# A linear-attention and gated-MLP kernel on one core: zeros by ScalarE, loads with their gaps, merged first loads, and a planner that counts instruction blocks

## The chip, the core and the metric

The kernel runs on one core of a Trainium2 chip. The core has five engines, each with its own queue of instructions, executed in order: TensorE (PE in the profile; its weight loads are shown as PEld), VectorE (DVE), ScalarE (ACT), GpSimd (POOL) and SyncE (SP), which here issues all copies between HBM and the on-chip memory. Engines wait for one another through semaphores. The metric is device time in microseconds, the median of several runs; lower is better.

## The reference

```python
for t in range(S):                      # S = 768, for 4 batches x 8 heads, head size 48
    kt, vt, bt = (k_n[:, :, t], v[:, :, t], beta[:, :, t, None])
    y[:, :, t] = np.einsum('bhd,bhde->bhe', q[:, :, t], state)
    v_old = np.einsum('bhde,bhd->bhe', state, kt)
    state = state + bt[:, :, :, None] * np.einsum('bhd,bhe->bhde', kt, vt - v_old)
...
x = attn_out.transpose(0, 2, 1, 3).reshape(B * S, H * D)     # 3072 tokens x 384
out = (x @ w_a * (x @ w_b)) @ w_out                          # 384 -> 1536 -> 384, float32
```

K is normalised per head and token. The first part is a recurrence over 768 tokens (a delta rule), the second a gated MLP without a non-linearity.

## The kernel before

**Tiling.** The 768 tokens are cut into 24 chunks of 32, and those into six groups of four. Within a chunk the recurrence is written as a triangular system, so that only 24 chunk steps are sequential. Four functions make the work of a group, and one that of the MLP:

- `weights(p)` loads a quarter or a half of the weights, which come as 64-bit floats, decodes them on VectorE to 32 bits (`decode`), takes a common scale from a Gram matrix on TensorE (`gram`, `total`), and splits each into two fp16 halves (`wsl`) or two F32R halves (`wo_hi`, `wo_lo`).
- `prep(g)` normalises K and scales, loads K and Q of a chunk with the feature dimension on partitions (`load_raw` into `raw0`, or into `raws`, a part of `wsl`, for the first group), multiplies by the norms (`rbk0`, which for later groups comes by way of a DRAM scratch `rk` and is spread over 64 partitions), splits into fp16 halves (`kqc`) and copies them into block matrices (`kqbd`).
- `solve(g)` inverts the triangular systems by elimination on VectorE, in tiles of the ring `b4` (one of which GpSimd clears first).
- `steps(g)` does the sequential steps: per chunk 48 + 24 + 48 + 24 tiny matmuls and 96 more that add to the state in the PSUM tile `S_ps`, with `tabd` as block matrix, and the chunk's tokens, split in fp16 halves, into `x`.
- `moe(s, ths)` does the MLP for a pair of chunks: 18 matmuls `bank<-x,wsl` of 256 columns, a product on VectorE (`g`), its split (`ghl`), and later 6 matmuls with `wo_hi` and `wo_lo`. This is most of TensorE's work; in this text it is the gated work.

The block matrices `kqbd` (4) and `tabd` (2) are zero outside their blocks. K and Q for two heads sit at partitions 0 to 47 and 64 to 111 of 112; the 16 between must be zero too. Before, GpSimd clears `raws`, three `kqbd` and both `tabd`, in 41 memsets, and VectorE the rest.

**The order.** Every operation is recorded in a list with an estimated duration (`price`), and `pack` simulates all engines: whenever an engine is free, it takes the ready operation of highest priority. That is done forwards and backwards in turn `PASSES` times, and the best order found is what each engine's queue then holds (`issue`, line 402, which is why nearly all rows of the profile have that line). `HOLD` lets a low-priority operation be held back for a short time for an urgent one. PSUM banks are given out by the same simulation. The estimated durations and the resulting order set everything; on the chip each engine follows its list.

Of the kernel before, what the change touches and what calls it, by code (L numbers as in the profile page):

```python
# [12 lines left out]
F32 = mybir.dt.float32  # L13
F32R = mybir.dt.float32r
F16 = mybir.dt.float16
I32 = mybir.dt.int32
# [6 lines left out]
B, H, S, D = 4, 8, 768, 48  # L23
DM, FF = 384, 1536
C = 32
NCH = S // C
P = 128
# [16 lines left out]


class Op:
    __slots__ = ("eng", "calls", "dur", "move", "rd", "wr", "deps", "pri", "at", "end", "tag", "stream", "banks", "cold", "use")

    def __init__(self, eng):
        self.eng, self.calls, self.dur, self.move = eng, [], 0.0, 0.0  # L50
        self.cold, self.use = 0.0, 0.0
        self.rd, self.wr, self.deps, self.tag, self.banks = {}, {}, set(), "", set()


class Plan:
# [89 lines left out]
    @staticmethod  # L145
    def price(eng, name, outs, ins, kw):
        out = outs[0]
        n = 1
        for d in out.shape[1:]:
            n *= d  # L150
        space = lambda a: getattr(a.tensor, "_space", None)
        wide = [a for a in ins if a.shape[-1] > 1 or len(a.shape) > 2]
        psum = any(space(a) == bass.MemoryType.PSUM for a in wide)
        if eng == "PE":
            k, m = ins[0].shape[0], ins[0].shape[-1]
            if min(k, m) <= 64:

                return 10.0 if k <= 64 else 17.0
            return (max(n, 60) / 2.4 + 2.3) * (4 if ins[0].dtype == F32 else 1)
        if eng == "ACT":  # L160
            extra = 93.0 * (hasattr(kw.get("scale"), "tensor") + ("accum_out" in kw))
            if name == "copy" and out.dtype == F16 and wide and wide[0].dtype == F16 and out.shape[0] == 32:
                extra += 105.0
            return (50 if psum else 93) + n / 1.2 + extra
        if eng == "DVE":
            speed, extra = 1.0, 61.0 * (n > 1 and any(a.shape[-1] == 1 and len(a.shape) == 2 for a in ins))
            if name == "tensor_reduce":
                n = 1
                for d in ins[0].shape[1:]:
                    n *= d  # L170
            elif name == "tensor_copy" and out.dtype == F16 and wide and wide[0].dtype == F16:
                speed, extra = 4.0, 95.0
            elif name.startswith("tensor_scalar") and not psum:
                speed = 2.0
            elif name == "memset":
                speed = 1.0 if out.dtype == F32 else 2.0
            elif name == "reciprocal":
                extra = 167.0
            return (66 + n / speed) / 0.96 + extra
        return 40 + n / 1.2  # L180

    def add(self, eng, fn, name, args, kw):
# [13 lines left out]
                self.open.append(op)  # L196
        op.calls.append((fn, args, kw, dict(self.lease)))
        if eng == "SP":
            op.dur = 475.0
            n = mybir.dt.size(outs[0].dtype)  # L200
            for d in outs[0].shape:
                n *= d
            op.move = max(n / 360.0, 20.0)
        else:
            dur = self.price(eng, name, outs, ins, kw)
            op.dur += dur
            if eng == "PE":
                n = -(-ins[0].shape[0] // 32) / 4
                op.use += dur * n
                if min(ins[0].shape[0], ins[0].shape[-1]) <= 64:  # L210
# [45 lines left out]
    def pack(self, pri, back=False):  # L256
# [6 lines left out]
        can = {e: [] for e in engs}  # L263
        free = {e: 0.0 for e in engs}
        ready, at, stop, done, dma = [0.0] * n, [0.0] * n, [0.0] * n, [], 0.0
        until, use, warm = self.WINDOW, 0.0, back
        vacant, held, blocked = [(k, {}) for k in range(len(self.pool))], {}, []
        for i, o in enumerate(ops):
            if not left[i]:
                heapq.heappush(wait[o.eng], (0.0, i))  # L270
        while len(done) < n:
# [31 lines left out]
                        vacant = [x for x in vacant if x[0] not in {k for _, k in at_[: len(need)]}]  # L303
            if i is None:
                continue
            o = ops[i]
            if not back and not o.banks and self.HOLD:

# [9 lines left out]
            if e == "PE" and not back:  # L318

                while until <= t:  # L320
                    warm = use > 0.43 * self.WINDOW if warm else use > 0.75 * self.WINDOW
                    use, until = 0.0, until + self.WINDOW
                took = o.dur if warm else o.cold
                full = took * o.use / o.dur
                part = min(1.0, (until - t) / took)
                use += full * part
                if part < 1.0:
                    warm = use > 0.43 * self.WINDOW if warm else use > 0.75 * self.WINDOW
                    use, until = full * (1 - part), until + self.WINDOW
            else:  # L330
                took = o.dur
# [10 lines left out]
            if e == "SP":  # L342
                if back:
                    end = t + o.dur + self.MOVE[0] + o.move + self.MOVE[1]
                else:
                    dma = max(dma, t + o.dur + self.MOVE[0]) + o.move
                    end = dma + self.MOVE[1]
            done.append(i)
            for k, late in nxt[i]:
                ready[k] = max(ready[k], end + late)  # L350
# [4 lines left out]

    MOVE = (900.0, 1100.0)
    SWITCH = 180.0
    HOLD = 300.0
    MARGIN = 5000.0
    WINDOW = 3413.0  # L360
    PASSES = 6

    def order(self):

# [41 lines left out]
def tile_kernel(ctx, tc, kqt, kn, vn, qtok, beta, wa, wb, wo, masks, out):  # L406
# [11 lines left out]
    scr = pool("scr", 1, space=bass.MemoryType.DRAM)  # L418
    psp = pool("ps", 1, space=PSUM)

    def ring(p, name, n, shape, dt):
        tiles = [p.tile(shape, dt, name=f"{name}_{i}") for i in range(n)]
        used = [0]

        def get():
            used[0] += 1
            return tiles[(used[0] - 1) % n]

        get.tiles = tiles
        return get  # L430
# [4 lines left out]
    b4 = ring(cst, "b4", 3, [P, 1024], F32)  # L435
# [32 lines left out]
    raws = wsl[:, 11:17].rearrange("p s d -> p (s d)").rearrange("p (c k a t) -> p c k a t", c=3, k=2, t=32)  # L468
    rawt = [raw0] + [raws[:, i] for i in range(3)]
    kn0 = wsl[:, 7:10].rearrange("p s d -> p (s d)").rearrange("p (c d) -> p c d", c=4)  # L470
    V.memset(rawt[0], 0.0)
    V.memset(kqbd[0], 0.0)
    G.memset(raws, 0.0)
    for t in kqbd[1:] + tabd:

        t = t.rearrange("p l i m -> p (l i m)" if len(t.shape) == 4 else "p a l q m -> p (a l q m)")
# [56 lines left out]
    def weights(p):  # L533
# [6 lines left out]
        for k in range(6):  # L540
            w, j = (wa, wb)[k // 3], k % 3
            if p == 0:
                if k % 2 == 0:
                    t = b4().bitcast(I32)
                t_ = t[:, 512 * (k % 2) : 512 * (k % 2) + 512]
            else:
                o = 2 * wd * (k % (1024 // wd))
                t_ = stage[:, o : o + 2 * wd]
            SP.dma_start(t_, w[j, :, col : col + wd].bitcast(I32))
# [111 lines left out]
    acc = [one(f"acc{i}", [P, DM]) for i in range(4)]  # L661

    def prep(g):
        chs = GROUPS[g]
# [7 lines left out]
        if g == 0:  # L672
# [1 line left out]
            A.activation(kn0, kn0, AF.Square)  # L674
            V.tensor_reduce(ss, kn0.rearrange("p c (q e) -> p (c q) e", e=D), AX.X, ALU.add)
            load_raw(0, raw0)
            for h2 in range(2):
                SP.dma_start(
                    raws[64 * h2 : 64 * h2 + D].rearrange("p c k a t -> p c (k a t)"),
                    kqt[1:4, h2].rearrange("c d x -> d c x"),  # L680
                )
        else:
            for ci, c in enumerate(chs):
                sq = ld()
# [28 lines left out]
        if g == 0:  # L713
# [1 line left out]
            for ci, c in enumerate(chs):  # L715
                gram(gb[:, 0:P], rawt[c][0:KR, 1].rearrange("p a t -> p (a t)"), ci == 0)
            for c in chs:
                SP.dma_start(acc[c], vn[c])
# [29 lines left out]
        for ci, c in enumerate(chs):  # L748
# [2 lines left out]
            rw, rb = (rawt[c], None) if g == 0 else (raw0, rbk0)  # L751
            if g:
                load_raw(c, rw)
                src = rk[:, ci * 8 : ci * 8 + 8].rearrange("h u r t -> h (u r t)")
                for h2 in range(2):
                    SP.dma_start(
                        rb[64 * h2 : 64 * h2 + 64].rearrange("p a t -> p (a t)"), src[h2].partition_broadcast(64)
                    )
            else:
                rb = abr()  # L760
                T.matmul(
# [396 lines left out]
def _layout(inputs):  # L1158
# [7 lines left out]
    kq = np.stack([tr(k), tr(q)], axis=4)  # L1166
    kqt = kq.transpose(5, 0, 3, 7, 1, 2, 4, 6)
    kqt = kqt.transpose(0, 2, 3, 6, 1, 4, 5, 7).reshape(NCH, 2, D, 1024)
    def natl(x):

        return x.reshape(B, 2, 4, NCH, C, D).transpose(3, 2, 4, 0, 1, 5).reshape(NCH, P, 384)
# [8 lines left out]
    for j in range(3):  # L1180
# [11 lines left out]
    masks[row, 32 + 2 * P + row % 8 * 2 + row // 64] = 1.0  # L1192
    masks[row, 48 + 2 * P + row // 8 % 4 * 2 + row // 32 % 2] = 1.0
    return {
        "kqt": f(kqt),
        "kn": f(natl(k)),
        "vn": f(natl(v)),
        "qtok": f(qtok),
# [23 lines left out]
```

## Time and profile before

| What | us |
|---|---|
| runs | 698.38, 713.67, 710.09; median 710.09 |
| profiled execution, its own time | 700.45 |
| its span (first to last instruction) | 698.7 |
| PE, DVE, ACT, POOL busy | 644.0, 553.3, 334.6, 27.5 |
| mean granted TensorE clock | 0.957 of full speed |

A row of a timeline is start, duration, engine, line, operation, output<-input and shapes, with a count and, in brackets, the idle time of the engine before it and what ended that. In a list of waits the columns are the total in us, the number of waits and the longest. "issue" is time in which an engine waited for nothing that the profile shows.

### The profile page before, as it was taken

To read this page: it belongs to the slowest core of one execution; us is meant where nothing else is said; L and a number is where in the kernel's file an instruction comes from. 1 tells how busy PE (TensorE), PEld (TensorE's weight loads), DVE (VectorE), ACT (ScalarE), POOL (GpSimd) and SP (SyncE) were. 2 spreads that over 40 slices of the span, in tenths; PEclk is the share of its full clock that TensorE was granted. 3 is DMA by queue.
4 is the path that set the end of the run, shared out by engine and by line. 5 is a ranking of instruction groups with operands and counts; after the bars stand their busy time and mean duration, and the time that the engine had idled before them with its cause. 6 is when DMAs were issued, how large, how long until landed. Compare 5 with 4: busy or idle time off the path is not lost.

```text
span 698.7 us, 25936 instructions
## 1 busy us (share of the span) xinstructions
PE 644.0 (92%) x11454; PEld 546.2 (78%) x11454; DVE 553.3 (79%) x1385; ACT 334.6 (48%) x786; POOL 27.5 (4%) x50
## 2 busy tenths in 40 slices
PE   2774999899989999999999998999899999999996
PEld 0443668788868888888888887888788888888886
DVE  8999889899657889998899997799797899643221
ACT  2374867655434446455545544445354334342222
POOL 9300000000000000000000000000000000000000
PEclk9976899999968999999999999999999999999999
DMA  9637756314212413243223232132231000100000
GB/s 228 179 111 215 220 151 195 101 35 136 71 60 69 111 40 100 63 106 92 71 69 96 56 100 81 46 92 76 72 88 49 2 22 27 37 26 1 12 13 23
DMA packets 32863, 58.36 MB, mean 84 GB/s; under 512 B 5104, under 2 KB 23280, under 8 KB 32752
## 3 DMA queue, kind: packets, MB, share of 16 engines
q1 hardware_dynamic: 32752, 56.72, 28.6%
q8 instruction: 89, 1.46, 0.9%
q14 instruction: 22, 0.18, 0.1%
HBM read 51.90 MB, written 4.80 MB: 81 GB/s over the span
## 4 chain that ended last, share of the span: by engine, by line
PE 81%; DVE 9%; DMA 5%; issue 3%; ACT 1%; SPq 0%; DVEq 0%; ACTq 0%
PE bank L402 78%; PE S_ps L402 3%; DMA wsl<-in_kqt 2%; DMA raw<-in_kqt 1%; DVE kqc L402 1%; DVE b L402 1%; DVE kqbd L402 1%; DVE wsl L402 1%; DVE tabd L402 1%; DVE x L402 1%; DMA b<-in_wa 1%; DMA t<-in_vn 1%; DVE raw L402 0%; DVE tmp L402 0%; DVE ghl L402 0%
## 5 line engine op out<-in xcount | busy, mean ns | idle before, releaser
L402 PE MATMUL bank<-x,wsl 128*128 128x256 f16 x2592 | 314.0, 275 | 1.7 <-issue 1.1
L402 PEld LDWEIGHTS <-wsl 128*128 128x128 f16 (+1 forms) x2676 | 249.4, 99 | 68.7 <-issue 22.7
L402 PE MATMUL bank<-wo_hi,ghl 128*128 128x384 f32 x576 | 187.4, 364 | 0.3 <-issue 0.2
L402 ACT COPY a<-bank 128x256 f32<-128x256 f32 x144 | 53.6, 372 | 141.3 <-PE bank L402 141.0
L402 PEld LDWEIGHTS bank<-wo_hi,ghl 128*128 128x128 f32 x576 | 107.9, 190 | 3.2 <-issue 0.6
L402 DVE TENSOR_TENSOR g<-bank,a 128x256 f32<-128x256 f32 x144 | 60.7, 421 | 59.8 <-ACT a L402 56.5
L402 PE MATMUL bank<-wo_lo,ghl 128*128 128x384 f32 x288 | 97.9, 340 | 0.0
L402 ACT CAST ghl<-g 128x256 fp32r<-128x256 f32 x144 | 58.1, 404 | 54.7 <-DVE g L402 54.0
L402 PEld LDWEIGHTS <-kqbd 112*64 112x64 f16 x3360 | 60.3, 115 | 17.7 <-issue 13.1
L402 DVE TENSOR_TENSOR ghl<-g,ghl 128x256 fp32r<-128x256 f32 x144 | 60.2, 419 | 14.9 <-ACT ghl L402 14.3
L402 PEld LDWEIGHTS bank<-wo_lo,ghl 128*128 128x128 f32 x288 | 55.2, 192 | 0.3 <-issue 0.2
L402 DVE TENSOR_TENSOR b<-b,tmp 128x31 f32<-128x31 f32 (+20 forms) x154 | 49.3, 320 | 2.1
L402 DVE TENSOR_TENSOR tmp<-b,b 128x31 f32<-128x31 f32 (+20 forms) x154 | 49.0, 318 | 2.1
L402 PE MATMUL bank<-shl,kqbd 112*64 112x48 f16 x2208 | 44.7, 192 | 0.6 <-issue 0.6
L402 DVE COPY tabd<-ta 32x1024 f16<-32x1024 f16 (+1 forms) x96 | 38.6, 402 | 5.4 <-PE bank L402 2.2
L402 PEld LDWEIGHTS <-tabd 128*128 128x128 f16 x1152 | 34.2, 97 | 5.4 <-issue 2.9
L402 ACT ACTIVATE ld<-ld 128x384 f32<-128x384 f32 x60 | 31.2, 522 | 12.9 <-DMA ld<-in_kn 11.0
L402 DVE COPY kqbd<-kqc 48x2048 f16<-48x2048 f16 x48 | 33.6, 701 | 3.1 <-PE bank L402 2.5
L402 PE MATMUL S_ps<-uhl,khl 32*48 32x48 f16 x2208 | 23.5, 186 | 8.8 <-issue 8.7
L402 PEld LDWEIGHTS <-khl 32*48 32x48 f16 x2208 | 20.3, 97 | 13.6 <-issue 12.7
L402 DVE TENSOR_TENSOR shl<-S_ps,shl 112x768 f16<-112x768 f32 x23 | 21.9, 953 | 6.6 <-ACT shl L402 6.5
L402 PE MATMUL bank<-kqc,kqbd 112*64 112x64 f16 x1152 | 23.4, 199 | 2.9 <-DVE kqbd L402 2.4
(138 smaller groups left out, 742.2 us busy)
## 6 DMA issues: line engine op xcount, KB each, us to landing
raw<-in_kqt SPq DMA_DIRECT2D x42, 192.0 KB, 3.7
rbk<-rk SPq DMA_DIRECT2D x40, 128.0 KB, 3.4
stage<-in_wo SPq DMA_DIRECT2D x12, 384.0 KB, 3.8
t<-in_vn SPq DMA_DIRECT2D x24, 192.0 KB, 2.5
t<-in_kn SPq DMA_DIRECT2D x24, 192.0 KB, 3.0
out<-wsl SPq DMA_DIRECT2D x24, 192.0 KB, 2.1
ld<-in_kn SPq DMA_DIRECT2D x20, 192.0 KB, 2.4
ld<-in_qtok SPq DMA_DIRECT2D x20, 192.0 KB, 2.4
```

Source lines behind the costliest of these rows:

```text
L402: fn(*(self.place(a, lease) for a in args), **{k: self.place(a, lease) for k, a in kw.items()})
```

## The change

It does five things.

1. **Zeros.** A one-column tile of zeros is set by VectorE, and ScalarE copies it, broadcast, over all six block matrices, in 24 copies of 512 fp32 columns. No memset of `raw0`, `raws`, `kqbd` or `tabd` is left.
2. **Loads with gaps.** The host lays K and Q out as 112 rows with the 16 zero rows in place, so a chunk comes in one copy of 112 rows and not in two of 48. The spread of the norms over 2 x 64 partitions is one copy, too.
3. **First loads.** The first quarter of each weight comes in one copy of three slabs (the ring `b4` is made of one tile for it), the first four chunks of V in one copy into `acc`.
4. **Planner: blocks.** `supply` follows TensorE's instructions (2 or 4 a matmul) through blocks of 256, with `FETCH` = 3600 ns between one block and the next. An operation that would wait over `STALL` = 150 ns for its block is passed over for another that is ready.
5. **Planner: the rest.** SyncE's copies wait for the eighth copy before them to land (`LANES`), an issue counts 430 and not 475 ns, F32R matmuls count as longer, `HOLD` is 0, and 12 passes are made instead of 6.

```diff
+        def supply(t, o, mark):
+
+            nonlocal began, issued
+            n, took = o.many, o.dur
+            k, end, last = issued, t, began
+            while n:
+                room = 256 - (k + self.SHIFT) % 256
+                j = min(room, n)
+                end += took * j / o.many
+                k, n = k + j, n - j
+                if j == room:
+                    last = end = max(end, last + self.FETCH)
+            if mark:
+                began, issued = last, k
+            return end
...
+                while supply(t, ops[j], False) - t - ops[j].dur > self.STALL and len(passed) < 12:
...
+                if self.FETCH:
+                    took = max(took, supply(t, o, True) - t)
...
+                    at[i] = t = max(t, landed[-self.LANES])
...
-    HOLD = 300.0
+    HOLD = 0.0
...
-    V.memset(rawt[0], 0.0)
-    V.memset(kqbd[0], 0.0)
-    G.memset(raws, 0.0)
-    for t in kqbd[1:] + tabd:
...
-        for i in range(0, 4096, 512):
-            G.memset(t[:, i : i + 512], 0.0)
+    zero = cst.tile([P, 1], F32, name="zero")
+    V.memset(zero, 0.0)
+    for t in kqbd + tabd:
...
+        for i in range(0, 2048, 512):
+            A.copy(t[:, i : i + 512], zero[0:n].broadcast_to([n, 512]))
...
+                if j == 0:
+                    SP.dma_start(t[:, k : k + 3], w[:, :, col : col + wd].bitcast(I32).rearrange("j p x -> p j x"))
...
-        for h2 in range(2):
-            SP.dma_start(rw[64 * h2 : 64 * h2 + D].rearrange("p k a t -> p (k a t)"), kqt[c, h2])
+        SP.dma_start(rw[0:KR].rearrange("p k a t -> p (k a t)"), kqt[c])
...
-                src = rk[:, ci * 8 : ci * 8 + 8].rearrange("h u r t -> h (u r t)")
-                for h2 in range(2):
-                    SP.dma_start(
-                        rb[64 * h2 : 64 * h2 + 64].rearrange("p a t -> p (a t)"), src[h2].partition_broadcast(64)
-                    )
+                src = rk[:, ci * 8 : ci * 8 + 8]
+                src = bass.AP(src.tensor, src.offset, [list(src.ap[0]), [0, 64], [1, 512]])
+                SP.dma_start(rb.rearrange("p a t -> p (a t)"), src)
```

On ScalarE, at its start. Before, the first work is the Square of the K rows (`wsl<-wsl`), then two small masks and the root of the sums:

```order
L402 ACT_TABLE_LOAD
L402 ACTIVATE wsl_101<-wsl_101 128x1536
L402 COPY a_0_96<-mk_100 128x256
L402 COPY a_1_97<-mk_100 128x256
L402 ACT_TABLE_LOAD
L402 ACTIVATE s0_120<-ss_119 128x32
L402 CAST kqc_0_79<-raw0_111 112x16x32
```

and now:

```order
L458 ACT_TABLE_LOAD
L458 COPY kqbd0_102<-zero_111 112x512 x4
L458 COPY kqbd1_103<-zero_111 112x512 x4
L458 COPY kqbd2_104<-zero_111 112x512
L458 ACTIVATE wsl_99<-wsl_99 128x1536
L458 COPY kqbd2_104<-zero_111 112x512 x3
L458 COPY kqbd3_105<-zero_111 112x512
L458 ACT_TABLE_LOAD
L458 ACTIVATE s0_119<-ss_118 128x32
L458 COPY kqbd3_105<-zero_111 112x512 x3
```

Nine copies of zeros now stand ahead of the Square, and four more ahead of the root.

On VectorE, at its start. `wsl<-b` rows decode weights, `ss<-wsl` is the sum over the squares:

```order
L402 MEMSET raw0_111 128x1024
L402 MEMSET kqbd0_104 112x2048
L402 TENSOR_SCALAR wsl_101<-b4_0_70 128x256
L402 SCALAR_TENSOR_TENSOR wsl_101<-b4_0_70,wsl_101 128x256 x2
L402 MEMSET S_ps_69 32x2x384
L402 TENSOR_SCALAR wsl_101<-b4_0_70 128x256
L402 SCALAR_TENSOR_TENSOR wsl_101<-b4_0_70,wsl_101 128x256
L402 TENSOR_SCALAR wsl_101<-b4_1_71 128x256
L402 TENSOR_REDUCE ss_119<-wsl_101 128x32
```

and now:

```order
L458 MEMSET zero_111 128x1
L458 MEMSET S_ps_69 32x2x384
L458 TENSOR_REDUCE ss_118<-wsl_99 128x32
L458 TENSOR_SCALAR wsl_99<-b4_70 128x256 x2
L458 SCALAR_TENSOR_TENSOR wsl_99<-b4_70,wsl_99 128x256
L458 TENSOR_SCALAR s0_119<-s0_119 128x32
```

The sum has moved ahead of all decoding, and the two memsets are gone.

On TensorE, where the place of the first long gap of the late part was (some 14,400 instructions in; `tabd` rows are the last of 24 tiny matmuls, `khl` rows the first of the 96 into the state):

```order
L402 LDWEIGHTS tabd_108
L402 MATMUL bank_68<-uhl_133,tabd_108 128x48
L402 LDWEIGHTS khl_127
L402 MATMUL S_ps<-uhl_133,khl_127 48x48
L402 LDWEIGHTS khl_127
```

and now:

```order
L458 LDWEIGHTS tabd_106
L458 MATMUL bank_67<-uhl_132,tabd_106 128x48
L458 MATMUL bank_68<-wo_hi,ghl_91 128x384
L458 MATMUL bank_68<-wo_lo,ghl_91 128x384
L458 MATMUL bank_68<-wo_hi,ghl_91 128x384
L458 LDWEIGHTS khl_126
L458 MATMUL S_ps<-uhl_132,khl_126 48x48
```

Three wide matmuls of the MLP now stand between the two runs of tiny ones.

More of the change, by code (lines that the diff above doesn't have):

```diff
@@ L46 @@
 class Op:
-    __slots__ = ("eng", "calls", "dur", "move", "rd", "wr", "deps", "pri", "at", "end", "tag", "stream", "banks", "cold", "use")
+    __slots__ = ("eng", "calls", "dur", "move", "rd", "wr", "deps", "pri", "at", "end", "tag", "stream", "banks", "cold", "use", "many")
     def __init__(self, eng):
         self.eng, self.calls, self.dur, self.move = eng, [], 0.0, 0.0
-        self.cold, self.use = 0.0, 0.0
+        self.cold, self.use, self.many = 0.0, 0.0, 0
         self.rd, self.wr, self.deps, self.tag, self.banks = {}, {}, set(), "", set()
@@ L209, in add @@
                 op.use += dur * n
+                op.many += 4 if ins[0].dtype == F32 else 2
                 if min(ins[0].shape[0], ins[0].shape[-1]) <= 64:
@@ L345, in pack @@
                 else:
+                    at[i] = t = max(t, landed[-self.LANES])
+                    free[e] = stop[i] = t + took
                     dma = max(dma, t + o.dur + self.MOVE[0]) + o.move
                     end = dma + self.MOVE[1]
+                    landed.append(end)
             done.append(i)
@@ L429, in ring @@
         get.tiles = tiles
+        get.whole = whole if joined else None
         return get
@@ L659, in low @@
         A.copy(dst, t.rearrange("p (a b) -> p a b", b=dst.shape[-1]) if len(dst.shape) == 3 else t)
-    acc = [one(f"acc{i}", [P, DM]) for i in range(4)]
+    accs = one("acc", [P, 4, DM])
+    acc = [accs[:, i] for i in range(4)]
     def prep(g):
```

69 lines of the change are left out of this document (51 added, 18 removed).

## The prediction

> **What bounds the kernel now.** I read the page first, then the busy time by stage, then TensorE's idle time, its timeline at the longest gaps and the clock there.
>
> ```profile
> span 698.7 us, 25936 instructions
> PE 644.0 (92%) x11454; PEld 546.2 (78%) x11454; DVE 553.3 (79%) x1385; ACT 334.6 (48%) x786; POOL 27.5 (4%) x50
> PEclk9976899999968999999999999999999999999999
> q1 hardware_dynamic: 32752, 56.72, 28.6%
> q8 instruction: 89, 1.46, 0.9%
> ```
>
> ```profile
> 0.00:97.40 97.40, 63.24 (x1179) 40.54 (x1179) 88.60 (x234) 53.67 (x124) 23.64 (x46) 0.85 0.67 188
> 97.40:194.50 97.10, 94.64 (x1567) 80.96 (x1567) 84.52 (x211) 59.62 (x140) 0.00 (x0) 0.97 0.38 110
> 194.50:223.40 28.90, 25.25 (x926) 20.85 (x924) 16.95 (x39) 11.75 (x27) 0.95 (x1) 0.70 0.23 61
> 223.40:630.80 407.40, 398.25 (x7296) 348.29 (x7297) 345.76 (x863) 191.74 (x453) 2.86 (x3) 0.99 0.24 66
> 630.80:698.70 67.90, 62.62 (x491) 55.59 (x489) 17.43 (x41) 17.81 (x45) 0.00 (x0) 0.98 0.04 12
> ```
>
> The second table gives, for each stretch, its length and the busy time of PE, PEld, DVE, ACT and POOL, then granted clock, DMA share and GB/s. Until 97.4 us (where the first pair of chunks is done and the gated matmuls can begin) VectorE is the bound: 88.6 of 97.4 us busy, TensorE 63. From 97.4 us on TensorE is: 94.6 of 97.1, 398 of 407. So a gain before 97.4 must come out of VectorE, and a gain after it out of TensorE's own gaps or its clock. Those gaps have one kind:
>
> ```profile
> PE S_ps L402 <- issue: 8.7, 5, 2.5
> PE bank L402 <- issue: 4.1, 6, 1.1
> ```
>
> ```profile
> 420.86 0.94 PE L402 MATMUL bank<-shl,kqbd 112*64 112x48 f16 x48
> 421.73 0.78 PE L402 MATMUL bank<-uhl,tabd 128*128 128x48 f16 x24
> 422.44 0.85 PE L402 MATMUL S_ps<-uhl,khl 32*48 32x48 f16 x84
> 425.74 0.26 PE L402 MATMUL S_ps<-uhl,khl 32*48 32x48 f16 x12 [2.46 <-issue]
> ...
> 496.76 0.23 PE L402 MATMUL S_ps<-uhl,khl 32*48 32x48 f16 x7 [2.34 <-issue]
> ```
>
> ```profile
> 198.30:214.90 16.60, 16.10 (x489) 13.06 (x490) 8.97 (x24) 5.31 (x13) 0.95 (x1) 0.50 0.23 62
> ...
> 426.50:429.90 3.40, 3.40 (x16) 2.71 (x14) 2.70 (x5) 2.34 (x6) 0.00 (x0) 0.50 0.02 5
> ...
> 498.20:501.60 3.40, 3.40 (x19) 2.33 (x16) 2.69 (x5) 0.06 (x1) 0.00 (x0) 0.50 0.01 5
> ```
>
> The wait "issue" sums to 12.8 us in 11 places. It falls inside a run of tiny matmuls that wait for nobody (84, then 2.46 us of nothing, then 12 more of the same). The page shows why: the instruction queue moved 89 packets, and TensorE ran 2 x 11454 = 22908 instructions, which is 257 a packet. TensorE's instructions come in blocks of about 256, and tiny matmuls use them up (48 + 24 + 84 with their loads, 312 instructions, in 2.4 us) before the next block has come. After the two late gaps the granted clock is 0.50 for 3.4 us each, after the one at 196.5 us for 16.6 us.
>
> **The zeros.** These rows carry the start (the first is VectorE's busy time in the first 10 us: stretch, busy, clock, DMA share, GB/s; in the others start, duration, engine, work, idle time before it):
>
> ```profile
> 0.00:10.00 10.00, 8.13 (x12) 1.00 0.83 253
> ...
> 1.01 0.91 DVE L402 MEMSET raw<- 128x1024 f32 x1 [1.01 <-PEq L1211]
> 2.30 1.76 DVE L402 MEMSET kqbd<- 112x2048 uint32 x1 [0.38 <-issue]
> ...
> 4.50 0.89 DVE L402 SCALAR_TENSOR_TENSOR wsl<-b,wsl 128x256 int32<-128x256 int32 x2
> ...
> 5.54 0.70 DVE L402 MEMSET S_ps<- 32x768 f32 x1 [0.15 <-issue]
> 5.78 1.48 ACT L402 ACTIVATE wsl<-wsl 128x1536 f32<-128x1536 f32 x1 [3.77 <-DMA wsl<-in_kn]
> ...
> 7.59 0.71 ACT L402 COPY a<-mk 128x256 f32<-128x256 f32 x2 [0.33 <-DMA mk<-in_masks]
> 7.91 1.73 DVE L402 TENSOR_REDUCE ss<-wsl 128x32 f32<-128x1536 f32 x1
> 8.32 1.28 ACT L402 ACT_TABLE_LOAD   x1
> ...
> 11.42 0.52 DVE L402 TENSOR_SCALAR neg<-mk 128x128 f16<-128x128 f32 x1
> ...
> 15.43 7.75 POOL L402 MEMSET tabd<- 128x512 f16 x16
> 15.50 6.07 DVE L402 TENSOR_SCALAR neg<-mk 128x128 f16<-128x128 f32 x1
> ...
> 20.66 0.91 DVE L402 MEMSET b<- 128x1024 f32 x1
> 21.65 0.62 ACT L402 CAST kqc<-raw 112x512 f16<-112x512 f32 x1 [11.75 <-DMA acc<-in_vn]
> ...
> 96.85 0.56 DVE L402 TENSOR_TENSOR x<-t,x 128x384 f16<-128x384 f32 x1
> ```
>
> Removed from VectorE: the memsets, 0.91 + 1.76 = 2.7 us. Removed from GpSimd: 41 memsets. While its last 16 ran, VectorE's cast to neg took 6.07 us, where the same form took 0.52 at 11.42 us. It ends at 21.6 us together with two neighbours and the 0.91 us memset, all of which would take about 2.6 us. If the hold goes, that is 6.1 - 2.6 = 3.5 us.
>
> Added to ScalarE: 24 copies of 512 fp32 columns. Between a 256-column copy (0.36) and a 512-column cast (0.62) I take 0.58: 13.9 us. Most lie in its 11.75 us of idle time, but nine stand ahead of the Square of the K rows, and the new order has VectorE's sum of those squares ahead of every weight decode. A table load of 1.3 us and nine copies from about 0.7 us on end at 7.2; the Square ends at 8.7, where it ended at 7.3. VectorE then has only the 0.70 us memset of the state's bank and so nothing from about 1.8 to 8.7 us: 6.9. The root waits for four more copies (2.3) and another table load, until 12.5, while VectorE has its sum (1.7) and three decode steps (about 1.2 by the 0.89 for two): 0.9 more. Before, VectorE was idle for 1.9 of its first 10 us, of which 1.0 before the first instruction. So the added wait is 7.8 - 0.9 = 6.9. Who is queued behind: the decodes, so the first Gram matmuls on TensorE, which idled there anyway. In both orders the write that frees the first gated matmul (the last row) is the 216th row on VectorE, so nothing else is shortened. Start: -2.7 - 3.5 + 6.9 = +0.7 us. Ends: -7 (no wait for the Square) to +7 (the hold was not GpSimd's and stays, and the wait is longer).
>
> **The loads.** SyncE issues fewer copies (K and Q 42 to 21, broadcasts 40 to 20, first weights 6 to 2, V 4 to 1).
>
> ```profile
> wsl<-in_kqt SPq DMA_DIRECT2D x2, 576.0 KB, 9.7
> b<-in_wa SPq DMA_DIRECT2D x3, 256.0 KB, 3.8
> rk<-rT SPq DMA_DIRECT2D x20, 4.0 KB, 2.1
> ...
> DMA to landing us min/median/max: 2.8/3.4/4.4
> ...
> DVE raw L402 <- DMA raw<-in_kqt: 4.0, 4, 1.3
> ```
>
> The first K and Q loads (48 rows at a time) took 9.7 us from issue; as 112 rows I expect less, but VectorE is late anyway, so 0; the same for the merged first weights, which land later than one slab did, while VectorE waits for the Square. If that cover is gone, they cost up to 3. Later K and Q loads: VectorE waited for them 4 times, 4.0 us; with one copy in place of two I take -1 (ends -4 and +1).
>
> The broadcast of the norms (rbk) has no row of its form: 128 KB copies from a 64-fold repeated row landed after 2.8 to 4.4 us; now 256 KB go in one copy whose source has an outer dimension of two. By the nearest row, the same copy at half size, the moved part is 3.4 - 2.1 = 1.3 us, doubled 4.7 to landing, about 1 us later than the pair's second half. Twenty of them, most with some slack, some used as soon as planned: +2 us. Low end 0. High end: if the two outer rows are what is divided over the 16 engines, each of two carries 128 KB; the hardware queue's mean is 56.72 MB in 28.6% of 16 engines x 698.7 us, 17.7 KB per us and engine, so 7.4 + 2.1 = 9.5 us to landing, 6 late.
>
> The Trainium skill says just that ("DMA: Bandwidth & Descriptors", the section on why a DMA increments its semaphore by 16): the number of engines is the largest up to 16 that divides the slowest dimension of both sides, here two. No run so far shows a copy with so small an outer dimension. By that rule the term is the high end, and the sum is that of the first rival.
>
> **The planner.** It now passes over a TensorE group whose block would run dry by over 150 ns, takes F32R matmuls as longer, holds nothing back, and counts eight DMA semaphores. I counted the order in blocks of 256 from the place of the gaps, with matmul times from the trace. The blocks before the two late gaps had 1.65 and 1.60 us of matmuls, and none of gated work; in the new order the blocks at those places have 3.2 and 4.3 us. So these gaps go: 2.46 + 2.34 = 4.8 us, and with them 2 x 3.4 us at half clock, 3.4 us. Of some sixty later blocks two remain short (2.1 and 2.6 us), for which I give back 1.5. The early gaps stay: between the last gated matmul of the first four chunks and the first of the next, both orders have no gated work to mix in (1838 TensorE instructions before, 1888 now, in the stretch 194.5 to 223.4 us). Sum of this part: -6.7; ends -14 (the 16.6 us at half clock go too, 8.3 more, less some) and 0.
>
> **Sum.** +0.7 + 0 - 1 + 2 - 6.7 = -5.0 against this execution's own 700.45 us (1.75 lie outside its span): 695.5. The median of the runs is 710.09; one run and the profiled execution are near 700, two runs at 710 and 714. I can't say which group the changed kernel's runs will be in, and add a quarter of the distance: **698 us**.
>
> **Rivals.**
> - Slower: the rbk copy on two engines. Twenty copies land 6 us later than planned. For: the source's outer dimension is two. Against: rbk0 is one buffer, refilled as soon as it is free, and many uses come later than that. In VectorE's order the use waits at the head, with the gate products behind it, and TensorE's banks wait for those. At 1 to 2 us for each of 20: 20 to 40 us, 715 to 735. It becomes slower than the 2% line from 1.4 us a copy.
> - Faster: ScalarE's copies are in time, so that VectorE's start gains its 6.2 us in full, and the long half-clock stretch at 198 us vanishes: 695.5 - 7 - 8 = 681. Against: the order on ScalarE.
> - The planner's count doesn't do what it says: the real blocks start elsewhere, gaps move and the clock dips stay: 695.5 + 6.7 = 702. For: the trace has short blocks without a gap too. The Trainium skill's "Runtime: NRT & Kernel Launch", section on instruction fetch, has the crossing of a block boundary "mostly hidden", by which there was nothing to gain; the 2.46 us row speaks against that here.
>
> **Chances.** The forecast 45% (by itself 688 to 708), two engines 20%, faster start and clock 17%, no effect of the planner 18%. A measurement of this kernel tells about 2% from no change, 14 us: below 696 is faster, above 724 slower. Faster: the second rival's 17% and 13% of the forecast, 30%. Slower: half of the first rival and a little of the others, 16%. Else 54%. A range from 682 to 720 leaves out the lower half of the fast rival and the upper part of the slow one.
>
> **What would show it.** In the profile after: VectorE idle between 2 and 8 us, and no 6 us cast near 15 us; TensorE's "issue" waits only before 235 us, with the clock at 1.00 around 425 and 500 us; time to landing of rbk near 4.7 us and VectorE's wait for it under 5 us in all. A landing of 8 to 10 us and VectorE waiting for rbk would make the first rival right; a first gated matmul before 93 us the second; "issue" gaps of 2 us after 400 us the third.

## The result, and the profile after

| Kernel | us | ratio to before, 95% interval |
|---|---|---|
| before (beside the changed kernel) | 698.38, 701.37, 710.09, 713.67 | |
| changed | median 733.79 (732.49 to 733.96) | 1.048 (1.044 to 1.052) |

The changed kernel is slower, outside the range, and inside that of the first rival (715 to 735 us). The medians of before stand at 696 to 703 us beside the experiments below; the ratios are to the before of the same chip. Runs that took over 1.5% longer than the fastest of their kernel (two of before's four here, one each of e7, e9, e12 and e14) are left out of the ratios and of the medians below, and e9 and e12, whose profile fell in such a run (granted clock 0.31 and 0.72), were run again as e18 and e13.

The page of the changed kernel answers those shown of before; its last line gives each engine's share of the chain that ended last, and the line of before's page for the same stands below it:

```profile
span 731.9 us, 25818 instructions
...
PE 654.5 (89%) x11454; PEld 550.8 (75%) x11454; DVE 542.6 (74%) x1384; ACT 344.5 (47%) x810; POOL 5.0 (1%) x9
...
PEclk9987768999996899998999999999999999999999
...
PE 39%; DVE 34%; DMA 17%; ACT 6%; issue 3%; SPq 0%; POOLq 0%; ACTq 0%; DVEq 0%
```

```profile
PE 81%; DVE 9%; DMA 5%; issue 3%; ACT 1%; SPq 0%; DVEq 0%; ACTq 0%
```

VectorE has less work than before (542.6 for 553.3 us) and the span is 33 us longer: nothing here is a sum of work. Copies stand in the chain for 17% of the span in place of 5%. By stage (stretch, its length, busy PE, PEld, DVE, ACT, POOL, granted clock, DMA share, GB/s), cut at the same gated matmuls as the table of before:

```profile
0.00:112.00 112.00, 73.17 (x1378) 47.19 (x1379) 83.18 (x243) 72.03 (x160) 1.16 (x5) 0.82 0.58 177
112.00:209.50 97.50, 90.04 (x1343) 76.15 (x1342) 79.00 (x200) 52.09 (x126) 0.00 (x0) 0.96 0.34 101
209.50:240.90 31.40, 24.98 (x951) 20.63 (x949) 20.61 (x45) 12.88 (x29) 0.95 (x1) 0.77 0.30 81
240.90:664.80 423.90, 403.69 (x7298) 351.23 (x7296) 342.36 (x858) 189.69 (x452) 2.86 (x3) 0.98 0.22 64
664.80:731.90 67.10, 62.60 (x491) 55.58 (x488) 17.44 (x41) 17.78 (x45) 0.00 (x0) 1.00 0.04 13
```

The first part, up to 2 us ahead of the first gated matmul in both, is 14.6 us longer (112.0 for 97.4), and VectorE, its bound, is busy for 83.2 us of it in place of 88.6: it waits. The fourth stretch is 16.5 us longer, with TensorE idle for 20.2 us of it where it was idle for 9.2. What VectorE and ScalarE wait for (total us, times, longest):

```profile
DVE raw L458 <- DMA raw<-in_kqt: 25.8, 7, 6.8
...
ACT kqc L458 <- DMA raw<-in_kqt: 16.1, 6, 4.6
...
DVE raw L458 <- DMA rbk<-rk: 12.8, 5, 5.2
```

In before the same three rows were 4.0 (shown in the prediction), 9.8 and 0.4 us:

```profile
ACT kqc L402 <- DMA raw<-in_kqt: 9.8, 9, 2.1
...
DVE raw L402 <- DMA rbk<-rk: 0.4, 1, 0.4
```

One such place, first in SyncE's timeline (its copies at their issue), then in VectorE's:

```profile
75.67 0.64 SPq L458 DMA_DIRECT2D rbk<-rk  x1
...
84.75 0.53 SPq L458 DMA_DIRECT2D rbk<-rk  x1
87.45 0.33 SPq L458 DMA_DIRECT2D stage<-in_wo  x1
87.88 0.37 SPq L458 DMA_DIRECT2D raw<-in_kqt  x1
```

```profile
84.03 0.69 DVE L458 TENSOR_TENSOR raw<-raw,rbk 112x512 f32<-112x512 f32 x1 [5.15 <-DMA rbk<-rk]
...
95.14 0.69 DVE L458 TENSOR_TENSOR raw<-raw,rbk 112x512 f32<-112x512 f32 x1 [3.12 <-DMA raw<-in_kqt]
```

The broadcast issued at 75.67 us frees the multiplication at 84.03. The next broadcast is issued at 84.75, as soon as that multiplication has read the one buffer, and the K and Q copy issued 3 us behind it lands at 95.1, 7.2 us after its issue. So there are two kinds of lateness: of the broadcast, and of the copy behind it. SyncE's queue is in order, and it stands in wait for broadcasts for 51.9 us in all (1.4 in e1 below), so what stands behind in that queue can be issued later, too; the experiments don't separate that part.

### The profile page after: what moved, and what is told of

The parts are those of the page before. It is cut to its first block, busy times and chain, and to the rows that moved or that the text cites. A ratio compares the mean times of both kernels' runs of the same rounds, so it can differ in the third digit from the quotient of the medians.

```text
span 731.9 us, 25818 instructions
## 1 busy us (share of the span) xinstructions
PE 654.5 (89%) x11454; PEld 550.8 (75%) x11454; DVE 542.6 (74%) x1384; ACT 344.5 (47%) x810; POOL 5.0 (1%) x9
## 4 chain that ended last, share of the span: by engine, by line
PE 39%; DVE 34%; DMA 17%; ACT 6%; issue 3%; SPq 0%; POOLq 0%; ACTq 0%; DVEq 0%
PE bank L458 38%; DMA raw<-in_kqt 5%; DVE b L458 5%; DMA rbk<-rk 4%; DVE wsl L458 3%; DVE g L458 3%; DVE kqbd L458 3%; DVE tmp L458 2%; DVE ghl L458 2%; DVE kqc L458 2%; DVE tabd L458 2%; DVE t L458 2%; DVE x L458 2%; DMA rk<-rT 2%; DMA ld<-in_qtok 2%
## 5 line engine op out<-in xcount | busy, mean ns | idle before, releaser
L458 PE MATMUL bank<-x,wsl 128*128 128x256 f16 x2592 | 317.5, 277 | 0.0
L458 PEld LDWEIGHTS <-kqbd 112*64 112x64 f16 x3360 | 63.9, 118 | 33.3 <-issue 24.5
L458 DVE TENSOR_TENSOR ghl<-g,ghl 128x256 fp32r<-128x256 f32 x144 | 60.5, 420 | 25.8 <-ACT ghl L458 25.8
L458 PE MATMUL bank<-shl,kqbd 112*64 112x48 f16 x2208 | 47.4, 193 | 13.8 <-DVE shl L458 8.1
L458 DVE TENSOR_TENSOR tmp<-b 128x31 f32<-128x31 f32 (+20 forms) x154 | 48.8, 317 | 2.0
L458 DVE TENSOR_TENSOR raw<-raw,rbk 112x512 f32<-112x512 f32 x20 | 13.8, 688 | 38.6 <-DMA raw<-in_kqt 25.8
L458 PE MATMUL bank<-kqc,kqbd 112*64 112x64 f16 x1152 | 25.1, 206 | 4.7 <-DVE kqbd L458 4.6
```

The source lines that it names most:

```text
L458: fn(*(self.place(a, lease) for a in args), **{k: self.place(a, lease) for k, a in kw.items()})
```

## The experiments

All 18 runs, with the median and the ratio to before (95% interval):

| Run | median, us | ratio |
|---|---|---|
| e1 changed, broadcasts in pairs, same order | 702.94 | 1.009 (1.006 to 1.012) |
| e2 before, broadcasts on 2 x 32 rows, same order | 722.52 | 1.036 (1.032 to 1.040) |
| e3 before, new planner | 712.14 | 1.021 (1.016 to 1.026) |
| e4 before, new zeros and loads, pairs | 693.91 | 0.994 (0.990 to 0.997) |
| e5 e4 and blocks | 692.86 | 0.995 (0.992 to 0.999) |
| e6 e4 and no hold | 694.31 | 0.994 (0.990 to 0.997) |
| e7 e4 and the new estimates | 699.65 | 1.004 (1.000 to 1.007) |
| e8 e1 without blocks | 703.09 | 1.008 (1.005 to 1.012) |
| e9 e1 and 20 spare copies | 740.60 | 1.063 (1.061 to 1.066) |
| e10 e1, broadcasts on 4 x 16 rows | 711.14 | 1.020 (1.017 to 1.023) |
| e11 e4 without the new zeros | 701.17 | 1.007 (1.005 to 1.009) |
| e12, e13 e4 with blocks and no hold | 685.82, 685.77 | 0.985 (0.982 to 0.988), 0.981 (0.977 to 0.985) |
| e14 e13 with the merged broadcast | 716.88 | 1.025 (1.020 to 1.031) |
| e15 e13, tiny matmuls planned longer | 694.26 | 0.993 (0.989 to 0.996) |
| e16 e13, F32R matmuls planned longer | 697.31 | 0.996 (0.993 to 0.999) |
| e17 e13 without the new zeros | 702.22 | 1.004 (0.998 to 1.011) |
| e18 as e9, one run | 740.33 | |

### The broadcast

e1 and e2 keep the order of their kernel word for word on every engine but SyncE, whose rows differ in the broadcasts alone. e1 is the changed kernel with

```diff
-                src = bass.AP(src.tensor, src.offset, [list(src.ap[0]), [0, 64], [1, 512]])
-                SP.dma_start(rb.rearrange("p a t -> p (a t)"), src)
+                with plan.group():
+                    for h2 in range(2):
+                        SP.dma_start(rb[64 * h2 : 64 * h2 + 64]..., src[h2].partition_broadcast(64))
```

> The changed kernel, with the broadcast of the norms issued again as two copies of 64 rows, recorded as one operation with the same planned duration, so that every engine's order stays word for word that of the changed kernel; only the 20 broadcasts differ. Theory A (a copy whose source has an outer dimension of two is carried by two DMA engines, lands 5 us late and holds up the copies queued behind it): landing back near 3 to 4 us, VectorE's waits for rbk and raw (12.8 and 25.8 us) down to under 5 in all, time 695 to 710. Theory B (the new order itself is longer, and the late copies lie beside other work): landing as in A, but the time stays above 722. Theory C (half and half): 710 to 722.

and e2 is the kernel before with

```diff
-                        rb[64 * h2 : 64 * h2 + 64]..., src[h2].partition_broadcast(64)
+                        rb[64 * h2 : 64 * h2 + 64]...,
+                        bass.AP(src[h2].tensor, src[h2].offset, [[0, 2], [0, 32], [1, 512]]),
```

> The kernel before, in its own order, with each of its 40 broadcasts of 128 KB written with a source of 2 x 32 rows in place of 64 (the same bytes to the same place). Theory A (the outer dimension sets the number of engines): each copy is carried by two engines and lands after 5 us or more, two of them per chunk one behind the other, VectorE waits for rbk and raw over 20 us, time 720 to 740. Theory B (the late copies cost little, the new order costs): under 710.

e10 writes e1's copies with a source of `[[0, 4], [0, 16], [1, 512]]`:

> The kernel of e1 in its own order, with the source of each 64-row broadcast written as 4 x 16 rows. If the outer dimension sets the number of engines, each 128 KB copy is carried by four, 32 KB each where two engines carried 128 KB of the merged copy: the pair (64 KB an engine, if both fall on the same four) lands after about 2.1 + 64/17.7 = 5.7 us by the rate in the profile of before, between the 3 of 16 engines and the 7 to 8 of two; time 706 to 718. If the number of engines isn't set so: 702 to 704, as e1.

e9 and e18 add to each of e1's pairs the changed kernel's merged copy, into a buffer that nobody reads:

```diff
+                    spare = scr.tile([P, 512], F32, name=f"spare{c}")
+                    SP.dma_start(spare, bass.AP(src.tensor, src.offset, [list(src.ap[0]), [0, 64], [1, 512]]))
```

> The kernel of e1 in its own order, and behind each of the 20 pairs of broadcasts one more copy in the changed kernel's form (2 x 64 rows of 2 KB, 256 KB) into a spare buffer that nobody reads or waits for. So what it adds is only what a two-engine copy does to the copies queued behind it. Theory A1 (the loss of the changed kernel is mostly the copies behind it: K and Q): 718 to 735, VectorE's wait for raw above 20 us. Theory A2 (the loss is the broadcast's own late landing): 700 to 708.

> The kernel of e9 once more, for its profile: 736 to 744. If the spare copies act on the copies behind them, VectorE waits for raw and ScalarE for raw longer than in e1 (11.4 and 9.6 us) by 15 us or more together, while the waits for rbk stay under 3. If they act by SyncE waiting for a copy's semaphore, the copies behind are issued late: the gaps between SyncE's issues and the landing counted from the issue tell which.

and e14 has the merged copy in the fastest order found:

> The kernel of e12 with the merged broadcast of the changed kernel (the order is planned anew with one copy in place of two, so it is not that of e12 word for word). If the two-engine copy costs what it cost in e1's order (31 us): 712 to 722. If it costs what it cost before's order (25 us): 706 to 716. If e12's order has more slack for late copies: under 700.

Without the merged copy and with nothing else changed, 733.8 us become 702.9: 31 us by the medians, 27 by the ratios (1.048 and 1.009). In before's own order the same bytes on 2 x 32 rows cost 25 us (722.5 beside 697.4), and between e13 and e14 it is 31 us, there with an order planned anew. Theory A held for the times of e1 and e2; of its other signs one failed: e1's waits for `rbk` and `raw` fell to 0.5 and 11.4 us, not under 5 in all. The semaphore records of the copies, grouped by kernel, tell the rest (copies, separate moments at which a copy's semaphore moved, us from issue to the last of them; then the same time for K and Q copies, those issued within 6 us behind such a copy and all others):

```
kernel   copy             moments   min / median / max     K, Q behind it   others
e1       40 x 128 KB      16        2.7 / 3.0 / 5.3        4.2 (7)          3.9 (14)
e10      40 x 128 KB       5        3.3 / 4.1 / 6.7        5.7 (7)          4.2 (14)
e2       40 x 128 KB       3        4.6 / 6.0 / 9.1        6.3 (28)         3.7 (14)
changed  20 x 256 KB       3        6.9 / 7.4 / 9.4        7.2 (7)          4.0 (14)
e18      spare, 256 KB     3        7.2 / 8.1 / 11.7       8.6 (6)          4.0 (15)
```

The moments follow the outer dimension of the source: 16, 4 and one more, 2 and one more. So does the landing, and not by size alone: the 128 KB of e2 land later than the 128 KB of e1. The copies behind are late by 1.5 us (e10) to 4.6 us (e18), though they are spread over 16 parts as before. A part of each waits on the two busy engines: in e18 the 14th moment of such a K and Q copy stands at 4.7 to 5.2 us in five of the six, and the last two at 8.1 to 9.3. e10's forecast landing was that of the pair, 5.7 us; counted from the issue of its first copy the pair lands after 5.6, and the time (711) is within the forecast.

e18 separates the two kinds. These are the waits of e1 and of e18, in the same order of work:

```profile
DVE raw L458 <- DMA raw<-in_kqt: 11.4, 7, 4.6
...
ACT kqc L458 <- DMA raw<-in_kqt: 9.6, 5, 2.9
...
DVE raw L458 <- DMA rbk<-rk: 0.5, 1, 0.5
```

```profile
DVE raw L458 <- DMA raw<-in_kqt: 35.2, 7, 8.7
...
ACT kqc L458 <- DMA raw<-in_kqt: 18.9, 6, 7.4
...
DVE raw L458 <- DMA rbk<-rk: 0.5, 1, 0.5
```

Nobody waits for the spare copy, and the broadcast itself is on time (0.5 us of waits in both), yet 38 us are lost (740.6 in e9 beside 702.9), more than theory A1 had (718 to 735). The K and Q copies land late: 33 us of added waits on VectorE and ScalarE. It is the landing that is late, and not the issue behind a wait of SyncE: SyncE waits for no spare copy, and for broadcasts 0.9 us. In the changed kernel both kinds are there: against e1, 12.3 us more on `rbk` (12.8 for 0.5) and 14.4 more on `raw` (25.8 for 11.4), 6.5 more on ScalarE. As spare copies add bytes of their own, e18 shows that the second kind is enough for a loss of this size, not how the 31 us divide.

### The planner

e3 is the kernel before with the whole new planner; e4 has the other half of the change, with pairs.

> The kernel before with the planner of the changed kernel alone (blocks, eight copies in flight, the new estimates, no hold, 12 passes); its zeros and its loads are those of before. If the planner's part is worth what was predicted (6.7 us): 690 to 698 beside 700 to 706 of before, and no gap called issue after 400 us. If it does nothing: 700 to 708. If the new order is itself the loss (theory B): over 715.

> The kernel before with the zeros on ScalarE, the K and Q loads of 112 rows and the merged first loads, but with the planner of before and with the broadcasts as pairs of 64 rows. By the terms of the prediction (+0.7 for the start, 0 and -1 for the loads): 698 to 708. If the wait for the Square is the loss at the start (theory B, first gated matmul later than 105 us): 710 or more.

The planner alone loses 15 us (712.1 beside 697.4; between the ranges of "does nothing" and of theory B), and it loses 9 from e4 to e1, where the pair is also planned as one copy. So an order that is longer in itself costs 9 to 15 us, beside the late copies of theory A, though less than theory B had. e4 itself, 693.9 us, is below its forecast of 698 to 708. Two parts do nothing by themselves: with the count of eight copies alone, or 12 passes alone, added to e4's planner, the order that comes out is that of e4 word for word. (Added to e13's planner, 12 passes do give another order; no run has it.) The other three were run one by one, as numbers in the planner:

```diff
-    HOLD = 300.0
+    HOLD = 0.0
...
-    FETCH = 0.0
+    FETCH = 3600.0
...
-                return 10.0 if k <= 64 else 17.0
+                return 10.0 if k <= 64 else 20.0
+            if ins[0].dtype == F32R:
+                return 34.0 + n / 2.4
...
-            op.dur = 475.0
+            op.dur = 430.0
```

> The kernel of e4 (data changes, pairs of 64 rows, planner of before) with the count of blocks added to the planner and nothing else of it: the hold of 300 ns, the old estimates and 6 passes stay. Theory P1 (the count of blocks is what loses the 9 us between e4 and e1, since groups that are passed over make the sequential steps late): 700 to 705, TensorE's waits for the step's operands (shl, fhl, uhl) longer. Theory P2 (it only removes the late gaps): 686 to 691, no gap called issue after 400 us. The gate of theory P3 (the hold or the estimates lose it) needs this one at or below 694.

> The kernel of e4 with the hold set to 0 and nothing else of the planner changed. Theory P3a (without the hold, long gated groups start just ahead of the urgent tiny ones, so that TensorE's next step comes late): 699 to 704, with more waits for shl and uhl. Theory P1 (blocks): 690 to 697, as e4.

> The kernel of e4 with the new estimates alone (tiny matmuls of over 64 rows 20 and not 17 ns, F32R matmuls longer, an issue 430 and not 475 ns). Theory P3b (the estimates lose it, by a first part in which the first gated matmul comes later than 104 us): 699 to 704. Theories P1 and P3a: 690 to 697.

> The kernel of e1 (the changed kernel with pairs of 64 rows, 702.9 us) with the count of blocks turned off and all else of the planner kept. Theory P1 (blocks lose it): 692 to 697, with the late gaps called issue back. Theory P3 (hold or estimates lose it): 702 to 710.

Blocks alone and no hold alone give e4's time (692.9, 694.3 beside 693.9), the estimates alone lose 6 us, and e1 without blocks loses as much as e1. So theory P1 fell. P2 had the mechanism of e5 right (no gap over 0.7 us called issue is left after 216 us) but not its time, 686 to 691. The estimates are what is left. e12 and e13 have the two others without them, e15 and e16 then add one estimate each:

> The data changes with pairs of 64 rows, the count of blocks and no hold, but the estimates of before: e1 without its estimates, the candidate for the fastest. If the estimates alone lose what e1 lacks against e4 (theory P3b): 688 to 694. If it takes blocks and no hold together: 700 to 704.

> The kernel of e12 once more, for its profile: 684 to 690. If blocks do what the planner says, no gap called issue after 300 us and a clock of 1.00 from there on; the middle (gated matmuls 864 to 1296) in 101 to 104 us, as without the new estimates.

> The kernel of e12 with tiny matmuls of over 64 rows planned at 20 and not 17 ns, nothing else. If this estimate is what loses time: 693 to 702, with the middle (gated matmuls 864 to 1296) at 108 us or more. If not: 684 to 691.

> The kernel of e12 with F32R matmuls planned at 34 ns more a piece, nothing else. If this estimate is what loses time: 693 to 702, with the middle at 108 us or more. If not: 684 to 691. If e15 and e16 both lose, or neither does, then no single estimate is at fault, and the order that comes out is a matter of chance.

Blocks and no hold together are the fastest kernel here, 685.8 us, 1.9% under before and faster than either range given for e12; either estimate loses on top of it, 8.5 and 11.5 us (e15's middle, 106.5 us, stayed under the 108 that was forecast). So no single estimate is at fault. Where the time lies is seen in two stretches, the gated matmuls 864 to 1296 of the 2592 `bank<-x,wsl`, which is the middle, and those from 1296 on (columns as in the table by stage), first of e13, then of e4, then of e1:

```profile
306.60:409.30 102.70, 101.11 (x2051) 88.98 (x2049) 96.18 (x242) 56.14 (x130) 0.95 (x1) 1.00 0.31 93
409.30:676.40 267.10, 266.52 (x4366) 234.65 (x4364) 188.45 (x463) 110.44 (x261) 0.95 (x1) 1.00 0.14 43
```

```profile
300.20:404.00 103.80, 101.18 (x2051) 89.48 (x2049) 96.00 (x234) 53.73 (x127) 0.95 (x1) 1.00 0.33 92
404.00:677.50 273.50, 268.46 (x4367) 236.38 (x4365) 191.71 (x471) 111.74 (x264) 0.95 (x1) 0.99 0.14 42
```

```profile
310.00:423.90 113.90, 107.14 (x2120) 93.05 (x2117) 100.33 (x249) 54.96 (x131) 0.95 (x1) 0.96 0.29 84
423.90:692.80 268.90, 265.31 (x4296) 233.22 (x4293) 186.09 (x456) 109.34 (x259) 0.95 (x1) 1.00 0.14 43
```

From 1296 on, both orders with blocks gain about what was forecast of them (6.7 us): 267.1 and 268.9 in place of 273.5 us (276.2 in before), TensorE idle for 0.6 us in e13 in place of 5. In the middle e1 loses more than that: 113.9 us with 6.8 idle and the clock at 0.96. That stretch takes 102 to 104 us in all six orders of e4's kind with the old estimates (e4, e5, e6, e11, e13, e17), and 106.5, 108.5, 110.6 and 113.9 in e15, e16, e8 and e1. Those four have 48 to 72 more tiny matmuls in the stretch, under 2 us by rows of the prediction (0.94 us for 48, 0.78 for 24). What TensorE waits for in the middle of e1 is the steps' state:

```profile
399.89 0.21 PE L458 MATMUL bank<-shl,kqbd 112*64 112x48 f16 x2
402.37 1.43 PE L458 MATMUL bank<-shl,kqbd 112*64 112x48 f16 x46 [2.26 <-DVE shl L458]
```

In the list of waits over the whole run, e1 and then e13 have:

```profile
PE bank L458 <- DVE shl L458: 5.0, 3, 2.3
```

```profile
PE bank L456 <- DVE shl L456: 0.6, 2, 0.3
```

In e1 the step stands where VectorE has not yet split the state; the wait costs its 2.26 us and the clock is then 0.50 from 402.2 to 409.0 us. Whether the estimates always lead there, or these four orders happened to, isn't settled: each run is one order. e3, with before's data, divides likewise: against before it loses 9 us ahead of the first gated matmul (108.6 for 99.4) and 9 in the middle (114.1 for 105.2), and gains 6 behind it. The issue of 430 ns was not tried alone.

### The zeros and the loads

e11 is e4, and e17 is e13, with the block matrices cleared as before (`raw0` and `raws` need no clearing in either):

```diff
-            A.copy(t[:, i : i + 512], zero[0:n].broadcast_to([n, 512]))
+            G.memset(t[:, i : i + 512], 0.0)
```

> The kernel of e4 without the zeros on ScalarE: GpSimd and VectorE clear the block matrices as before (raw0 and raws need no clearing, since the gaps come with the load). If the zeros on ScalarE are worth about nothing, as predicted (+0.7): 692 to 697, as e4 (693.9). If the hold of VectorE by GpSimd's memsets is worth its 3.5 us: 696 to 700. If the wait for the Square costs more than that: 686 to 691, with the first gated matmul before 101 us.

> The kernel of e12 with the block matrices cleared by GpSimd and VectorE as before. If the zeros on ScalarE gain 7 us, as between e4 and e11: 691 to 696, with VectorE's 6 us cast near 15 us back. If that gain belonged to one order: 683 to 689.

The zeros on ScalarE gain 7 us in one order (701.2 to 693.9) and 16 in the other (702.2 to 685.8); e11 and e17 are both slower than every range given for them. VectorE's timeline of e11 shows one cause (GpSimd's follows):

```profile
6.82 1.75 DVE L456 TENSOR_REDUCE ss<-wsl 128x32 f32<-128x1536 f32 x1 [2.97 <-ACT wsl L456]
...
10.99 7.33 DVE L456 TENSOR_SCALAR wsl<-b 128x256 int32<-128x256 int32 x1
18.24 0.58 DVE L456 TENSOR_SCALAR s<-s 128x32 f32<-128x32 f32 x1
```

```profile
0.73 11.45 POOL L456 MEMSET kqbd<- 112x512 f16 x24 [0.29 <-POOLq L1270]
12.12 7.62 POOL L456 MEMSET tabd<- 128x512 f16 x16
```

A decode step, 0.48 us in the rows of before, takes 7.33 us while GpSimd clears, and with the zeros on ScalarE no such row is left. The loads alone (e11) give nothing over before (701.2 beside 696.4). Without `raws`, GpSimd's memsets begin earlier, and VectorE's hold is 7.33 and not 6.07 us; the rest of these 5 us is not explained. In e17 the first gated matmul begins at 113.2 us, in e13 at 100.0; 5.4 of these 13 us stand already where VectorE first writes the tile `zi` (24.64 and 19.26 us); the rest comes later, in an order planned anew.

## Why the prediction was wrong

Told in the order before, e4, e1, changed, the medians are 697.4 - 3.5 + 9.0 + 30.9 = 733.8 (before's is that beside e1 and e4; by the ratios the last step is 27). The forecast had -0.3 for the first step, -6.7 for the second and +2 for the third, and 2.5 for the spread. Without the merged copy the kernel is e1, 702.9 us, which the range would have held, but by luck: the second step has the wrong sign.

**The broadcast (+2; 31 measured) is the step that failed.** The prediction took "by the nearest row, the same copy at half size", about 4.7 us to landing, and kept the two engines as high end and as the slower rival with 20%. The landing was 7.4 us in the median, nearer to the high end than to 4.7, and the rival's 715 to 735 holds the result, though its landing of 8 to 10 us was too long: part of the loss came by a way that it hadn't priced. The row it was taken from was the nearest in bytes, not in the dimension that was changed. The Trainium skill ("DMA: Bandwidth & Descriptors", section on why a DMA increments its semaphore by 16) had the number of engines as the largest up to 16 that divides the slowest dimension of both sides, and says that the issuing sequencer adds the other 16 - k at once while each engine adds one when its part has landed. The trace agrees: one moment and two for an outer dimension of two, one and four for four, 16 for 64 rows.

**What the high end left out.** It priced the broadcast's own lateness. The copies queued behind, K and Q above all, are late as well (7.2 for 4.0 us), and over half of VectorE's added wait is on them (14.4 us beside 12.3 on the broadcasts, against e1). What stood against the rival, that "rbk0 is one buffer, refilled as soon as it is free", speaks for it: `raw0` and `rbk0` are one buffer each, so the four multiplications of a group follow one another through two landings. From the first to the last multiplication of a group it takes 205.7 us in e1 and 220.8 in the changed kernel, summed over the five groups.

**The planner (-6.7; +9 to +15 measured).** Its mechanism was right: in e13 no gap over 0.7 us called issue is left after 216 us, and the clock is 1.00 from 224 to 684 us; from gated matmul 1296 on, 9.1 us are gained over before (267.1 for 276.2), where 6.7 was forecast. In the changed kernel the gaps of 2.46 and 2.34 us are gone too; the longest called issue after 400 us are 1.10 and 0.96. But the prediction wrote "takes F32R matmuls as longer" and gave the estimates no term at all. Between e13 and e1 lie 17 us (685.8 and 702.9): e1 has the new estimates, the 12 passes, the count of eight copies and the pair planned as one copy. The runs show of these only that two estimates, each alone, lose 8.5 and 11.5 us. Nor did it say what would be late next: the split of the state for the next step, `shl`, before which TensorE now stops. In the changed kernel the clock drops at 427.8 us behind this row, near before's 426.5:

```profile
426.15 0.91 PE L458 MATMUL bank<-shl,kqbd 112*64 112x48 f16 x46 [1.75 <-DVE shl L458]
```

**The start (+0.7).** Its rows came as said; VectorE's timeline in the changed kernel:

```profile
8.21 1.75 DVE L458 TENSOR_REDUCE ss<-wsl 128x32 f32<-128x1536 f32 x1 [6.49 <-ACT wsl L458]
...
11.81 0.18 DVE L458 TENSOR_SCALAR s<-s 128x32 f32<-128x32 f32 x1 [1.11 <-ACT s L458]
...
18.96 0.21 DVE L458 TENSOR_SCALAR neg<-mk 128x128 f16<-128x128 f32 x1
```

The waits for the Square and the root are 7.6 us (7.8 forecast), and the cast is at 0.21 us: the hold was GpSimd's. Its size was too small. The 3.5 us were those of before's order; with the loads of the change the hold would have been 7.33 us, and e11 and e17 give 7 and 16 us for the zeros, with what the order adds. The prediction also counted the write that frees the first gated matmul as the 216th row in both orders. By the trace it is VectorE's 233rd instruction before and its 245th in the changed kernel, and even in e1 the first gated matmul begins at 106.7 us, where it began at 99.4.

**The loads (0 and -1).** Not seen apart from the order: e11, which also keeps the hold, is 0.7% slower than before. No run tells the two loads from each other.

**The rivals.** The faster one fell: the first gated matmul begins at 114.0 us, not before 93. The third, a planner without effect, fell too: the order had an effect, of the other sign.

## What to carry to other kernels

When a copy is merged, look at the outer dimension of both sides first, and take its price from a row with the same outer dimension; if there is none, plan with the bound, and not with the nearest row by bytes. A slow copy must be charged to those queued behind it as well: spare copies that nobody waited for cost 38 us, the late ones 31. A planner's estimates are part of the change: two new ones gave orders 8.5 and 11.5 us longer, so they are tried one at a time.

## What the runs showed of the hardware

A copy on few engines delays the well-spread copies behind it: K and Q landed 7.2 us after issue behind the merged broadcast and 4.0 elsewhere. One decode step of 0.48 us stood for 7.33 us on VectorE, some 15 of GpSimd's memsets at 0.48 us each (7.62 / 16). The Trainium skill ("SBUF — State Buffer", the section on its two separate sides) has the port pair that VectorE and GpSimd share held for one whole instruction, while the other is blocked. The trace agrees that one is blocked, but for many instructions in a row.
